# Linear attention and a squared-ReLU MLP on one core: query loads moved up, output stores moved to the SyncE queue, and a margin on every transfer in the kernel's own planner

## The chip, the cores and the metric

The kernel runs on one core of a Trainium2 chip. The time is the device time of one execution in microseconds. The kernel before took 288.01 us, the median of three executions (287.98 to 288.55). One further execution was profiled; it took 291.93 us, and its span in the trace is 290.2 us.

A core has TensorE (matmul, "PE" in the profile, with the weight loads as "PEld"), VectorE ("DVE"), ScalarE ("ACT"), GpSimd ("POOL") and SyncE ("SP", which only issues transfers). Transfers are issued on queues by SyncE, GpSimd or ScalarE, and 16 DMA engines carry them out.

## The reference

Eight batches of eight heads, 576 positions, head size 64. Attention is linear: with r = relu(x), the features of queries and keys are r·cos and r·sin of the position, so no softmax and no 576 x 576 matrix occurs. Then each position's 512 numbers go through an MLP with relu squared.

```python
batch, n_heads, seq, head_dim = (8, 8, 576, 64)

def phi(x, c, s):
    r = np.maximum(x, 0.0)
    return np.concatenate([r * c, r * s], axis=-1)      # 64 -> 128 features
q_p = phi(q, cos_w, sin_w)
k_p = phi(k, cos_w, sin_w)
kv = np.einsum('bhsf,bhsd->bhfd', k_p, v)
z = np.sum(k_p, axis=2)
num = np.einsum('bhsf,bhfd->bhsd', q_p, kv)
den = np.einsum('bhsf,bhf->bhs', q_p, z)[..., None] + 1e-06
attn_out = num / den

x = attn_out.transpose(0, 2, 1, 3).reshape(B * S, H * D)   # 4608 x 512
h = x @ w_in                                               # 512 -> 2048
r = np.maximum(h, 0.0)
return (r * r) @ w_out                                     # 2048 -> 512
```

Inputs and output are float32; the kernel multiplies in bf16.

## The kernel before

A batch has 512 positions in four pieces of 128 (j = 0 to 3) and a tail of 64 (j = 4), which has tensors of its own (kt, vt, qt, kpt, qpTt, xTt and so on). For each batch the steps are:

1. load k, v and q (1 MB each) and their tails;
2. features of k and q on ScalarE and VectorE (kp, qp), and a cast of v (vx);
3. "kz": the product of keys and values on TensorE, into kvz;
4. queries transposed (qp to qpT), from batch 2 on by a DMA transpose on the SyncE queue;
5. "num": qpT times kvz on TensorE, then the division on VectorE, which gives x;
6. x transposed (x to xT), from batch 2 on by a DMA transpose on the SyncE queue;
7. first MLP product (w1), relu and square (gT); from batch 3 on by Strassen's seven products, with sums of blocks in xs, w1s, rs;
8. second MLP product (w2), from batch 2 on (half of batch 1 too) by seven products per pair of row blocks ("pair"), with sums of blocks in gs and w2s, results in ysb;
9. store of ysb.

While TensorE does steps 7 and 8 of one batch, the other engines prepare the next two. Nobody writes that interleaving by hand: the kernel holds a planner. Each operation is declared with the engines that could do it, a guessed cost in us, what it reads and writes, and, for TensorE, a place in time. The planner then runs a list schedule with its guesses, chooses buffers, and emits all instructions in the order found. On the chip each engine takes its own instructions in that order and waits where data are missing.

```python
    def plan(self, t0):
        # (cut: takes, again and again, the operation that can start first)
            o.eng, o.start, o.end = e, s, s + o.engs[e]
            o.done = o.end + (o.lat if o.lat is not None else 0.17 if e == "PE" else 0.09) + self.HOP
            if o.size:                       # a transfer: one pipe for all
                pipe = o.done = max(o.end + o.land, pipe) + o.size
                if o.held is not None:
                    o.end = max(o.end, o.done - o.held)
            clock[e] = o.end
```

`size` is the guessed time of a transfer in the pipe (3.4 us for 1 MB), `land` a guessed latency. Loads, transposes and stores have a size, and so do the four loads of w1, which the hand-written prologue has issued before and which the planner only gets told of:

```python
    given = lambda keys, t, **kw: add(("GIVEN", 0.0), lambda _: None, w=keys, pos=t, **kw)
    for i in range(4):
        given([("w1", i)], 12.2, size=2.6)
    # (cut)
    t0 = {"PE": 16.8, "ACT": 17.3, "DVE": 17.1, "SP": 10.0, "POOL": 20.0, "GIVEN": 0.0}
```

The first operations after the prologue are declared in these lines (batch 0; `declare_plain` is the first MLP product without Strassen, `hb` its block of the hidden layer):

```python
    for j in (2, 3, J):
        for c in "cs":
            declare_feature("q", 0, j, c, DVE1 if c == "c" else ACT1)
        t = {2: 17.5, 3: 18.0, J: 27.0}[j]
        declare_qT_pe(0, j, t, BOTH)
        declare_num(0, j, t + 2.0)
        declare_xT_pe(0, j, t + 4.0, BOTH)
    for s in range(8):
        for i in range(2):
            declare_plain(0, s % 4 * 4 + 2 * i, s // 4, T1[0] + s * 2 * PROD2 + i * PROD2, s == 0)
```

The loads, the attention of batches 4 to 7 and the stores:

```python
    def declare_load(b, nm, eng, pos=None, after=()):
        # (cut) the main part, then the tail, each an operation of the queue `eng`
            add((eng, cost), load, w=[buf], pos=pos, size=size, after=after)

        # in declare_qT: a DMA transpose; `turned` remembers it
        turned["q", b, i] = add(("SP", 1.7 if n == 2 else 1.2), qT, r=keys, w=[dst], land=1.6, held=2.0, ...)

        # in declare_pair: the store of two row blocks, or of two sets of tails
        def store(_):
            if pair < 2:
                put(b, 2 * pair, at(y), n=2, eng=nc.gpsimd)
            else:
                for i in range(2):
                    put_tails(four(b) * 2 + i, at(y)[:, i])
        add(("POOL", 0.6), store, r=keys(0) + keys(1), size=1.7)

    for b in range(2, B):
        # (cut) first MLP product of batch b
        if b + 2 < B:
            for nm in "kv":
                declare_load(b + 2, nm, "SP", after=[turned["q", b + 1, J // 2]])
            declare_load(b + 2, "q", "SP", after=[turned["x", b + 1, J // 2]])
            declare_att(b + 2, T2[b] + 5.5, [T1[b + 1] + 0.3 + 1.75 * j for j in range(NS)])
        for i, pair in enumerate(PAIRS[b]):
            declare_pair(b, pair, T2[b] + i * 7 * PROD2)
```

`declare_att(b, kpos, npos)` gives TensorE's places for kz (`kpos`) and for the five num steps (`npos`). T1[b] and T2[b] are the places where the first and second MLP product of batch b begin. There is one buffer each for k, v and q (and for each tail), two for ysb, two for qpT, four for xT. The very last pair (batch 7, pair 1) stores its four quarters on SyncE (three) and ScalarE (one), in both versions.

Of the kernel before, what the change touches and what calls it, by code (L numbers as in the profile page):

```python
# [19 lines left out]
class Buf:  # L20


    def __init__(self, pool):
        self.pool, self.i, self.users = pool, None, 0
# [10 lines left out]
class Planner:  # L35
# [7 lines left out]

    HOP = 0.07

    def __init__(self, pools, window, in_turn):
        self.in_turn = in_turn
        self.free = {p: [(0.0, i) for i in range(n)] for p, n in pools.items()}
        self.window = window
        self.ops, self.writer, self.readers = [], {}, {}  # L50
        self.turns = {}
# [6 lines left out]
    def add(self, engs, fn, r=(), w=(), pos=None, lat=None, size=None, after=(), land=2.2, held=None):  # L58
        if isinstance(engs, tuple):
            engs = {engs[0]: engs[1]}  # L60
        if size:
            lat = land + size
        op = Op(engs, fn, pos, lat, size)
        op.land, op.held = land, held
        for k in r:
            if k in self.writer:
                op.deps.add(self.writer[k])
            self.readers.setdefault(k, []).append(op)
        for k in w:
            if k in self.writer:  # L70
                op.deps.add(self.writer[k])
            op.deps.update(x for x in self.readers.get(k, ()) if x is not op)
            self.writer[k], self.readers[k] = op, []
        for k in list(r) + list(w):
            b = k[0] if isinstance(k, tuple) else k
            if isinstance(b, Buf) and b not in op.bufs:
                op.bufs.append(b)
                b.users += 1
        op.after = set(after) - op.deps
        op.deps |= op.after  # L80
        self.ops.append(op)
        return op
# [27 lines left out]
    def plan(self, t0):  # L110
        ops = self.ops
        for n, op in enumerate(ops):
            op.n = n
            for d in op.deps:
                d.succ.append(op)
        pe = sorted((o for o in ops if "PE" in o.engs), key=lambda o: (o.pos, o.n))
        t = t0["PE"]
        for o in pe:
            o.late = o.slot = t
            t += o.engs["PE"]  # L120
        for o in reversed(ops):
            d = max(o.engs.values()) + (o.lat or 0.16)
            for s in o.succ:
                o.late = min(o.late, s.late - d)
            if "PE" not in o.engs:
                ends = [
                    s.slot + s.engs["PE"]
                    for s in o.deps
                    if "PE" in s.engs and any(b in s.bufs for b in o.bufs if b.pool in "FB")
                ]  # L130
                if ends:
                    o.late = min(o.late, max(ends) + 1.0)
        clock = dict(t0)
        waiting = {o: len(o.deps) for o in ops}
        pipe = 0.0
        ready = {e: [] for e in clock}
        order = []

        def arm(o):
            for e in o.engs:  # L140
                ready[e].append(o)

        for o in ops:
            if not o.deps:
                arm(o)
        left = len(ops)
        head = 0
        while left:
            best = None
            while head < len(pe) and pe[head].start is not None:  # L150
                head += 1
            for e in clock:
                cand = []
                for o in ready[e]:
                    if e == "PE" and o.slot > pe[head].slot + self.window:
                        continue
                    s = max(clock[e], o.pos if e not in ("PE",) and o.pos else 0.0)
                    for d in o.deps:
                        ordered = d in o.after or d.eng == e and e in ("PE", "ACT", "DVE")
                        s = max(s, d.end if ordered else d.done)  # L160
                    s = self.room(o, s)[0]
                    if s is not None:
                        cand.append((s, o))
                if not cand:
                    continue
                s0 = min(c[0] for c in cand)
                s, o = min(
                    (c for c in cand if c[0] <= s0 + 1e-9),
                    key=lambda c: (c[1].slot if e == "PE" else c[1].late, c[1].n),
                )  # L170
                if best is None or s < best[0]:
                    best = (s, e, o)
            if best is None:
                stuck = [o for o in pe if o.start is None][:6]
                raise RuntimeError(f"stuck: {[(o.fn.__name__, o.pos, o.n) for o in stuck]}")
            s, e, o = best
            for x in o.engs:
                ready[x].remove(o)
            o.eng, o.start, o.end = e, s, s + o.engs[e]
            o.done = o.end + (o.lat if o.lat is not None else 0.17 if e == "PE" else 0.09) + self.HOP  # L180
            if o.size:
                pipe = o.done = max(o.end + o.land, pipe) + o.size
                if o.held is not None:
                    o.end = max(o.end, o.done - o.held)
            clock[e] = o.end
            for b, i in self.room(o, s)[1]:
                b.i = i
                self.free[b.pool] = [f for f in self.free[b.pool] if f[1] != i]
            for b in o.bufs:
                b.users -= 1  # L190
                b.last = max(getattr(b, "last", 0.0), o.done)
                if b.users == 0:
                    self.free[b.pool].append((b.last, b.i))
            for x in o.succ:
                waiting[x] -= 1
                if not waiting[x]:
                    arm(x)
            order.append(o)
            left -= 1
        return order  # L200
# [3 lines left out]
def kernel(  # L204
# [82 lines left out]
    def at(buf, name=None):  # L287
        return mem[name or buf.pool][:, buf.i]
# [67 lines left out]
    def put(b, tt, y, c0=0, c1=DM, eng=None, n=1):  # L356
        dst = bass.AP(
            tensor=out.tensor,
            offset=(b * S + tt) * DM + c0,
            ap=[[J * DM, P], [1, n * DM if n > 1 else c1 - c0]],  # L360
        )
        eng.dma_start(out=dst, in_=y.rearrange("p i c -> p (i c)") if n > 1 else y[:, c0:c1])  # L362

    def put_tails(m, y):
        for i in range(2):
            dst = bass.AP(
                tensor=out.tensor,
                offset=((2 * m + i) * S + MAIN) * DM,
                ap=[[DM, TAIL], [1, DM]],
            )  # L370
            nc.gpsimd.dma_start(out=dst, in_=y[i * TAIL : (i + 1) * TAIL, :])

# [30 lines left out]


    LOAD = 3.4
    T_MM, T_MM128, T_MM65, T_TR = 0.1092, 0.0586, 0.0296, 0.066
    plan = Planner(POOLS, 4.5, ("gs1", "gs2", "gs3", "gs4"))
    add = plan.add  # L410
    PROD1, PROD2 = 4 * T_MM, 8 * T_MM

# [439 lines left out]
    def four(b):  # L852
        return 0 if b < 7 else 1
# [12 lines left out]
    def w2_keys(i, j):  # L866
        return [("w2", 2 * i + n) for n in range(2)]

    def declare_pair(b, pair, t):
        A, Bk, E = plan.buf("F"), plan.buf("B"), plan.buf("F")  # L870
        u = plan.buf("u")
# [61 lines left out]

        def store(_):
            if pair < 2:
                put(b, 2 * pair, at(y), n=2, eng=nc.gpsimd)
            else:
                for i in range(2):
                    put_tails(four(b) * 2 + i, at(y)[:, i])

        add(("POOL", 0.6), store, r=keys(0) + keys(1), size=1.7)

    def declare_rows(b, tiles, t, f_banks):

# [212 lines left out]
    for b in range(2, B):  # L1157
        if b > 2:
            if b in SEVEN:
                declare_x_sums(b)  # L1160
                for r in range(4):
                    declare_seven1(b, r, T1[b] + r * 7 * PROD1)
            for m, first, n in TAILS[b]:
                for i in range(first, first + n):
                    declare_tails(m, 2 * i, T2[b] - 1.5 + 0.01 * i)
        if b + 2 < B:
            for nm in "kv":
                declare_load(b + 2, nm, "SP", after=[turned["q", b + 1, J // 2]])
            declare_load(b + 2, "q", "SP", after=[turned["x", b + 1, J // 2]])
            declare_att(b + 2, T2[b] + 5.5, [T1[b + 1] + 0.3 + 1.75 * j for j in range(NS)])  # L1170
        for i, pair in enumerate(PAIRS[b]):
            declare_pair(b, pair, T2[b] + i * 7 * PROD2)

# [34 lines left out]
```

## Time and profile before

| | before |
|---|---|
| timed executions, median (range) | 288.01 us (287.98 to 288.55) |
| span of the profiled execution | 290.2 us |
| TensorE busy | 273.7 us, 94% |
| VectorE busy | 219.8 us, 76% |
| ScalarE busy | 192.6 us, 66% |
| GpSimd busy | 39.4 us, 14% |
| moved by DMA | 53.02 MB, mean 183 GB/s |
| 1 MB loads on SyncE, median issue to landing: k, v, q | 6.8, 10.2, 6.4 us |
| 512 KB stores on GpSimd, median issue to landing | 4.9 us, 15 of them |
| DMA transposes, median issue to landing: qpT, xT | 6.1, 5.4 us |

How to read the lines that follow. A group line names the source line, the engine, the operation, what it writes and reads (`qpT<-qp`), and how many. In the waits, "PE banks L401 <- DMA qpT<-qp: 4.5, 3, 2.8" says that TensorE's instructions of line 401 (its matmuls, all through one helper) waited for a transfer from qp to qpT: 4.5 us in total, three times, the longest 2.8. In a timeline each line has the start in us, the time it took, the engine, and what it did; a bracket at the end is the idle time of that engine before it and what ended it. SPq is SyncE's queue: the time there is that of issuing, and the transfer lands later.

### The profile page before, as it was taken

What the parts mean: (1) busy time and instruction counts of PE and PEld (TensorE: products, weight loads), DVE (VectorE), ACT (ScalarE), POOL (GpSimd) and SP (SyncE); (2) the same over time, 40 slices, a digit from 0 to 9 for tenths busy, and PEclk for the clock granted to TensorE, in tenths of its full rate; (3) what the DMA queues carried; (4) which work ended last, traced back from release to release, by engine and by line L of the source; (5) the groups of instructions that cost most, each with busy time, mean ns of one, the idle gap of its engine ahead of it and who ended that gap; (6) DMA issues with size and microseconds to landing.
All of it is one profiled execution on the core that took longest, in us unless ns stands there. A gap on an engine that the chain in (4) does not pass through costs nothing.

```text
span 290.2 us, 7068 instructions
## 1 busy us (share of the span) xinstructions
PE 273.7 (94%) x2827; PEld 225.6 (78%) x2827; DVE 219.8 (76%) x512; ACT 192.6 (66%) x379; POOL 39.4 (14%) x67
## 2 busy tenths in 40 slices
PE   8999999999999899589999999997999999999994
PEld 3678755887689788377788888976889888888883
DVE  2859999988845886389977799679974999169661
ACT  4676924897965877459946995689834853585521
POOL 8834345100000000000000000000013000100021
PEclk9999999999999999999999999999999999999999
DMA  7999999799999959999599866998096500110015
GB/s 247 289 207 320 324 242 388 175 171 325 237 189 267 230 163 138 218 312 161 101 189 291 217 188 116 275 288 202 9 224 97 136 3 0 75 72 2 1 75 145
DMA packets 77569, 53.02 MB, mean 183 GB/s; under 512 B 52032, under 2 KB 73024, under 8 KB 77536
## 3 DMA queue, kind: packets, MB, share of 16 engines
q1 hardware_dynamic: 67856, 29.76, 47.6%
q0 software_dynamic: 9536, 22.68, 26.9%
q8 instruction: 22, 0.36, 0.5%
q14 instruction: 11, 0.09, 0.1%
q10 hardware_dynamic: 144, 0.13, 0.1%
HBM read 36.70 MB, written 9.44 MB: 159 GB/s over the span
## 4 chain that ended last, share of the span: by engine, by line
PE 53%; DVE 17%; DMA 16%; POOL 4%; ACT 3%; SPq 3%; issue 3%; DVEq 0%; POOLq 0%; ACTq 0%
PE banks L401 52%; DVE gT L390 6%; DMA kt<-in_k_dram 6%; DMA qt<-in_q_dram 4%; DMA qpT<-qp 4%; DVE rs L393 3%; DMA k<-in_k_dram 2%; DVE gs L398 2%; SPq L329 2%; DVE w1s L398 2%; POOL w1sb L344 1%; DVE qp L379 1%; DVE kp L379 1%; SPq L337 1%; ACT rs L387 1%
## 5 line engine op out<-in xcount | busy, mean ns | idle before, releaser
L401 PEld LDWEIGHTS <-w1sb 128*128 128x128 bf16 x784 | 73.0, 98 | 11.3 <-issue 2.4
L401 PE MATMUL banks<-xT,w1sb 128*128 128x256 bf16 (+1 forms) x576 | 68.4, 267 | 1.0 <-DVE x L599 0.4
L401 PEld LDWEIGHTS <-gs 128*128 128x128 bf16 x480 | 46.5, 98 | 7.4 <-DVE gs L398 1.2
L401 PE MATMUL banks<-w2sb,gT 128*128 128x256 bf16 (+1 forms) x304 | 50.2, 306 | 0.8 <-ACT banks L905 0.5
L401 PEld LDWEIGHTS <-gT 128*128 128x128 bf16 x408 | 38.4, 98 | 13.6 <-issue 1.3
L387 ACT ACTIVATE rt<-banks 128x512 bf16<-128x512 f32 x64 | 37.7, 601 | 14.1 <-PE banks L401 9.4
L362 POOL DMA_DIRECT2D out_dram<-ysb x15 | 8.1, 541 | 213.4 <-DVE ysb L398 92.1
L401 PEld LDWEIGHTS <-w1s 128*128 128x128 bf16 x320 | 30.6, 98 | 7.1 <-issue 3.3
L401 PE MATMUL banks<-w2sb,gs 128*128 128x256 bf16 x240 | 30.9, 273 | 0.4 <-DVE ysb L398 0.4
L393 DVE CUSTOM_DVE_ANT_0 rs<-banks,sums 128x512 bf16<-128x512 f32 x40 | 27.2, 686 | 4.6 <-ACT sums L800 3.6
L401 PE MATMUL banks<-w2s,gs 128*128 128x256 bf16 x240 | 30.0, 273 | 0.5 <-DVE gs L398 0.3
L390 DVE TENSOR_TENSOR gT<-rs 128x1024 bf16<-128x1024 bf16 (+1 forms) x50 | 28.3, 580 | 1.6 <-ACT rs L387 0.8
L390 DVE TENSOR_TENSOR gT<-rt 128x512 bf16<-128x512 bf16 x48 | 19.9, 422 | 12.2 <-ACT rt L387 11.7
L398 DVE TENSOR_TENSOR ysb<-banks,sums 128x256 f32<-128x256 f32 x30 | 12.7, 422 | 19.5 <-ACT sums L914 9.1
L387 ACT ACTIVATE rs<-banks 128x512 bf16<-128x512 f32 x40 | 23.4, 610 | 3.7 <-PE banks L401 3.7
L401 PE MATMUL banks<-xs,w1s 128*128 128x256 bf16 x160 | 23.7, 273 | 0.8 <-ACT banks L793 0.8
L401 PE MATMUL banks<-xT,w1s 128*128 128x256 bf16 x160 | 22.3, 272 | 1.5 <-DVE rs L393 1.5
L377 ACT ACTIVATE qp<-q,sin_col 128x512 bf16<-128x512 f32 x32 | 22.9, 735 | 1.1 <-DMA q<-in_q_dram 1.1
L377 ACT ACTIVATE kp<-k,sin_col 128x512 bf16<-128x512 f32 x32 | 22.7, 738 | 0.2 <-DMA k<-in_k_dram 0.2
L599 DVE TENSOR_TENSOR x<-banks,den 128x512 bf16<-128x512 f32 x30 | 20.7, 692 | 1.0
L398 DVE TENSOR_TENSOR gs<-gT 128x1024 bf16<-128x1024 bf16 x26 | 17.9, 689 | 1.6 <-PE banks L401 1.1
L800 ACT COPY sums<-banks 128x512 f32<-128x512 f32 x20 | 11.9, 593 | 6.4 <-PE banks L401 6.1
(106 smaller groups left out, 377.6 us busy)
## 6 DMA issues: line engine op xcount, KB each, us to landing
out_dram<-ysb POOLq DMA_DIRECT2D x15, 512.0 KB, 4.9
k<-in_k_dram SPq DMA_DIRECT2D x6, 1024.0 KB, 6.8
v<-in_v_dram SPq DMA_DIRECT2D x5, 1024.0 KB, 10.2
q<-in_q_dram SPq DMA_DIRECT2D x5, 1024.0 KB, 6.4
v<-in_v_dram POOLq DMA_DIRECT2D x3, 1024.0 KB, 10.5
w1sb<-in_moe_w_in_dram POOLq DMA_DIRECT2D x4, 512.0 KB, 11.4
w2sb<-in_moe_w_out_dram POOLq DMA_DIRECT2D x4, 512.0 KB, 13.0
q<-in_q_dram POOLq DMA_DIRECT2D x2, 1024.0 KB, 9.5
```

Source lines behind the costliest of these rows:

```text
L329: eng.dma_start(out=main[:, :, js, :], in_=src[b, :, 0:MAIN, :].rearrange("h (p j) d -> p h j d", j=J)[:, :, js, :],)
L337: eng.dma_start(out=tail[g * TAIL : (g + 1) * TAIL, :, :], in_=src[b, g * HH : (g + 1) * HH, MAIN:S, :].rearrange("h p d -> p h d"),)
L362: eng.dma_start(out=dst, in_=y.rearrange("p i c -> p (i c)") if n > 1 else y[:, c0:c1])
L377: nc.scalar.activation(out=dst, in_=src, func=ACTF.Relu, scale=col)
L379: nc.vector.tensor_scalar(out=dst, in0=src, scalar1=0.0, scalar2=col, op0=ALU.max, op1=ALU.mult)
L387: nc.scalar.activation(out=out, in_=in_, func=ACTF.Relu)
L390: nc.vector.tensor_tensor(out=out, in0=in_, in1=in_, op=ALU.mult)
L393: nc.vector._custom_dve(TENSOR_ADD_SAT, out=out, in0=in0, in1=in1, s0=float("inf"), s1=0.0)
L398: nc.vector.tensor_tensor(out=out, in0=in0, in1=in1, op=op)
L401: nc.tensor.matmul(out=out, lhsT=lhsT, rhs=rhs, start=start, stop=stop, skip_group_check=True)
L599: nc.vector.tensor_tensor(out=x_at(b, j).rearrange("p (b k) (l d) -> p b k l d", b=n, l=2), in0=n4[:, :, :, 0:D].rearrange("p b (k l) d -> ...
L800: add(("ACT", 0.5), lambda _: nc.scalar.copy(out=at(u3), in_=bank(Bk)), r=[Bk], w=[u3])
```

## The change

Four things change together. The planner gets a margin: it takes every transfer to be of use 2.0 us later than it would compute, so what depends on a transfer is put later ("care on every transfer"). The queries of batches 4 to 7 are loaded together with keys and values instead of after the last transpose of x of the batch before. The stores of batches 2 to 7 go to the SyncE queue, where loads and transposes stand in line too, instead of to GpSimd's. And the places of kz and num for batches 4 to 7 are written anew: num 2.3 us earlier (LATER = -2.0 in place of +0.3), kz relative to the first product that follows. The aim is that fewer of TensorE's steps wait for a transfer, and that stores don't share the DMA engines with transposes that TensorE needs soon.

```diff
-    def __init__(self, pools, window, in_turn):
+    def __init__(self, pools, window, in_turn, margin):
+        self.margin = margin
@@ in plan
             if o.size:
-                pipe = o.done = max(o.end + o.land, pipe) + o.size
+                pipe = max(o.end + o.land, pipe) + o.size
+                o.done = pipe + self.margin
                 if o.held is not None:
-                    o.end = max(o.end, o.done - o.held)
+                    o.end = max(o.end, pipe - o.held)
@@
-    plan = Planner(POOLS, 4.5, ("gs1", "gs2", "gs3", "gs4"))
+    LATER = -2.0
+    plan = Planner(POOLS, 4.5, ("gs1", "gs2", "gs3", "gs4"), 2.0)
@@
+    def st_name(b):
+        return "SP" if b >= 2 else "POOL"
+    def st_eng(b):
+        return nc.sync if b >= 2 else nc.gpsimd
@@ in declare_pair (put_tails takes the engine too)
-                put(b, 2 * pair, at(y), n=2, eng=nc.gpsimd)
+                put(b, 2 * pair, at(y), n=2, eng=st_eng(b))
-                    put_tails(four(b) * 2 + i, at(y)[:, i])
-        add(("POOL", 0.6), store, r=keys(0) + keys(1), size=1.7)
+                    put_tails(four(b) * 2 + i, at(y)[:, i], st_eng(b))
+        add((st_name(b), 0.6), store, r=keys(0) + keys(1), size=1.7)
@@ in the loop over batches
-            for nm in "kv":
+            for nm in "kvq":
                 declare_load(b + 2, nm, "SP", after=[turned["q", b + 1, J // 2]])
-            declare_load(b + 2, "q", "SP", after=[turned["x", b + 1, J // 2]])
-            declare_att(b + 2, T2[b] + 5.5, [T1[b + 1] + 0.3 + 1.75 * j for j in range(NS)])
+            declare_att(b + 2, T1[b + 1] - 7.5, [T1[b + 1] + LATER + 1.75 * j for j in range(NS)])
```

More of the change, by code (lines that the diff above doesn't have):

```diff
@@ L362, in put, with put_tails @@
         eng.dma_start(out=dst, in_=y.rearrange("p i c -> p (i c)") if n > 1 else y[:, c0:c1])
-    def put_tails(m, y):
+    def put_tails(m, y, eng):
         for i in range(2):
@@ L370, in put_tails @@
             )
-            nc.gpsimd.dma_start(out=dst, in_=y[i * TAIL : (i + 1) * TAIL, :])
+            eng.dma_start(out=dst, in_=y[i * TAIL : (i + 1) * TAIL, :])
     def relu_scale(eng, dst, src, col):
```

## The prediction

> **What bounds the kernel now.** I read the page's first two parts, then the waits of TensorE, then TensorE's timeline around the idle stretches, then what stood on the SyncE queue there. The page first:
>
> ```profile
> PE 273.7 (94%) x2827; PEld 225.6 (78%) x2827; DVE 219.8 (76%) x512; ACT 192.6 (66%) x379; POOL 39.4 (14%) x67
> ...
> PE   8999999999999899589999999997999999999994
> ...
> DMA  7999999799999959999599866998096500110015
> ```
>
> TensorE is busy for 273.7 of 290.2 us, so everything that a schedule can win lies in its 16.5 us of idle time, and some of that is start and end. The holes show in the slices: an 8 and a 5 in slices 16 and 17 (109 to 123 us), a 9 or less near 190 to 200. Which wait ends last there is told by TensorE's own waits:
>
> ```profile
> PE banks L401 <- DMA qpT<-qp: 4.5, 3, 2.8
> PE banks L401 <- DVE rs L393: 1.5, 2, 0.9
> ...
> PE banks L401 <- DMA w1sb<-in_moe_w_in_dram: 0.3, 2, 0.2
> ```
>
> 4.5 us of it, in three waits, is for the transposed queries (qpT), which a DMA transpose on the SyncE queue makes. The timeline of TensorE places them, and places the smaller waits about 20 us earlier:
>
> ```profile
> 98.50 1.91 PE L401 MATMUL banks<-xT,w1sb 128*128 128x256 bf16 x16 [0.41 <-DVE x L599]
> 100.99 0.32 PE L401 MATMUL banks<-kvz,qpTt 128*64 128x65 bf16 x8 [0.59 <-ACT rt L387]
> ...
> 120.19 0.42 PE L401 MATMUL banks<-kvz,qpT 128*128 128x65 bf16 x8 [2.81 <-DMA qpT<-qp]
> ...
> 124.08 0.42 PE L401 MATMUL banks<-kvz,qpT 128*128 128x65 bf16 x8 [1.48 <-DMA qpT<-qp]
> ```
>
> Two holes, 2.81 and 1.48 us, belong to batch 4 alone. (The third, 0.21 us at 150.54, is batch 5's.) The reason stands on the two issuing queues:
>
> ```profile
> 103.87 0.58 SPq L329 DMA_DIRECT2D q<-in_q_dram  x1
> 104.50 1.29 SPq L337 DMA_DIRECT2D qt<-in_q_dram  x2
> 107.40 1.35 SPq L627 DMA_TRANSPOSE xT<-x  x1
> 111.34 8.43 SPq L538 DMA_TRANSPOSE qpT<-qp  x2
> ```
>
> ```profile
> 111.74 0.53 POOL L362 DMA_DIRECT2D out_dram<-ysb  x1 [24.63 <-ACT sums L909]
> 117.51 0.53 POOL L362 DMA_DIRECT2D out_dram<-ysb  x1 [5.24 <-DVE ysb L398]
> ```
>
> The queries of batch 4 are asked for only at 103.87 and land at about 110; their features are ready at 111.3; and 0.4 us after the first transpose is issued, GpSimd issues a 512 KB store of batch 2 on another queue. By the trace's landings this store took 8.2 us (the median is 4.9), the first transpose 8.8 us and the second 10.6 us (median 6.1). Batch 6, whose store was issued after both transposes, had 4.5 and 4.8 us and no hole.
>
> **What the Trainium skill says.** "DMA: Bandwidth & Descriptors", section "Queues, rings and completion order": a DMA engine takes turns between the queues that have work for it, a packet at a time, and takes one queue's descriptors in their order. Section "Issuing engines are not separate DMA queues" of the same page: whoever issues, the same 16 engines do the work and the transfers interleave. The trace agrees: store and transposes of batch 4 were both slow while they overlapped. On one queue the store would start behind or ahead of the transposes. "Perfetto Trace Analysis", section "Summary: the profiler window per engine type": for a DMA issued by SyncE the slice is generation and push, not the movement; the trace agrees (slices of 0.58 us, landing 6.4 us later), so I go by landings.
>
> **The change part by part.** The kernel's planner decides the order, so I read the built order of both versions. TensorE's instructions are the same in number and kind; only their order differs. I count places in TensorE work (8 matmuls of 128x256 take 0.87 us in the timeline, 8 of 128x65 take 0.24), from 16.8 us on.
>
> *Queries with keys and values.* In the old order the load of q for batches 4 to 7 may be issued 11 to 19 us of TensorE work after those of k and v, with 4.6 us left until VectorE comes to the first q feature of batch 4. In the new order it stands next to k and v, with 16.3 us. For batch 3 the old kernel already does so: k issued at 64.22, all three tensors with tails landed by 78.25, 14.0 us. So the wait on late queries goes. In its place the tails of k and v, which stand behind q, land about 3.2 us later (k and v of batch 4 landed 3.2 us apart, 1 MB each). Against this VectorE reaches the tail of k later: 96.3 to 99.4 for batch 4, 178.6 to 181.7 for batch 7. Net near zero for batch 4; for batch 7, whose loads are also issued 2 us earlier, some gain, because there the tail at 194.9 us held VectorE 0.9 us, and TensorE lost 0.78 and 0.90 us at 199.7 and 201.2 behind it. I put 0.6 us on batch 4 (half of 0.41 + 0.59 + 0.16) and 1.0 on batch 7.
>
> *Stores on SyncE.* 19 transfers move, 11 of 512 KB and 8 tails of 128 KB. GpSimd issued them at 0.53 us each and is otherwise idle, so taking them off it wins nothing. On SyncE the two stores of batch 2, 3 and 4 stand together behind the transposes of x and ahead of the next batch's query transposes, 12 us of TensorE work or more before them, and 3 to 10 us after TensorE has made their data: SyncE should not stand still for them, and they no longer meet the transposes. The two ysb buffers come free later, but the next pair writes them more than 15 us of work later. At the end four tail stores are issued on SyncE just before the last stores; the last one of all is on ScalarE (issued at 287.25), so nothing is lost.
>
> *The numerators and the margin.* LATER puts the numerators 2.3 us earlier, the 2 us margin holds them back behind their transposes. From the place where the first transpose of q may be issued to the first numerator there are now 8.3, 10.8, 9.0 and 15.2 us for batches 4 to 7 (before 7.9, 8.1, 8.1, 13.1). In the trace the issue came 2 to 3 us after that place and an undisturbed transpose took 4.5 to 6.1 us: 6.5 to 9 us. So the 2.81 + 1.48 + 0.21 = 4.5 us should go nearly whole, as the store is out of the way: I take 4.3.
>
> *The start.* The margin also falls on the four w1 loads, of which the planner knows only a guessed time. It believes w1 2 us later, and so puts the query transposes of pieces 2 and 3 of batch 0 before the first up-projection. But w1's first quarter was there at 16.24 us, and the transposes wait for ScalarE's features at about 17.6 and 18.3. In the old trace TensorE did 24 matmuls of 128x128 by then (24 x 0.0586 = 1.41 us) and ended the transposes at 18.86. In the new order it ends them at about 18.75 with those 24 still to do: 1.3 us lost. The 0.19 + 0.15 us waited for w1 later go: 1.0 us net loss, and TensorE is busy without a hole from there to 98 us but for 0.22 us, so it stays.
>
> Sum in the profiled run: -4.3 - 0.6 - 1.0 + 1.0 = -4.9 us. But the timed runs are at 288.01 while the profiled execution took 291.93, 3.9 us more. Some of the profile's waits must then be shorter or absent in the timed runs, those on transfers most likely. I count half of the three gains, 2.95 us, against the 1.0 lost, and leave 0.4 us for new small waits of a new order: 288.0 - 2.95 + 1.0 + 0.4 = 286.4. With the gains whole it is 288.0 - 4.9 + 0.4 = 283.5. I settle between, nearer to the first: 285.6.
>
> **The rivals.** (a) The stores become the bound of SyncE: each waits in line, and everything behind it waits too. For: the queue's own instructions already take 1.2 to 6 us per transpose, and issuing the two tails of k 2.2 to 4.1 us, so the queue is crowded around each load. Against: the built order has them after their data by 3 to 10 us of TensorE work (batches 2 to 4). It would give back 2 to 4 us: 288 to 290. (b) The tails of k land too late with q before them, and VectorE, which works in order, stands still with squares behind the tail feature: up to 2 us in each of batches 4 to 7, 290 or more. Against: the 3.1 us by which the feature is placed later. (c) The hole at 120 us is a thing of the profiled run. Then the change only costs its start: 288.5 to 289. (d) VectorE and ScalarE set the pace in 130 to 210 us (busy 9 or more of 10 us in several stretches), so holes that close at 120 open later as waits for rs and banks: gain 1 us, 287.
>
> **Range and chances.** The middle case is 285.6; (d) and half of (c) give the upper end 288.2, the gains whole 283.5, with luck 283.2. Faster by over 2% needs under 282.3, which asks for 5.7 us where the waits that the change touches come to some 7 us in all, less the start: 6%. Slower by over 2% needs 293.8, which only (a) and (b) together reach: 2%.
>
> **What would show it.** Right: no wait of TensorE for qpT over 0.5 us; landings of the query transposes at 4.5 to 6.5 us for batches 4 to 7; the first w1 matmul after about 18.7 us instead of 16.2; stores on SyncE issued with no wait of SyncE for y. Wrong: SyncE waiting for ysb before a transpose, VectorE waiting for kt or q by more than 1.5 us, or the hole before batch 4's numerators still there.

## The result, and the profile after

The changed kernel takes 283.94 us (median of four executions, 283.72 to 285.48) against 288.19 us of the kernel before, measured beside it (287.98 to 288.55). The ratio is 0.9863, with a 95% interval of 0.9826 to 0.990: 1.4% faster. The profiled execution of the kernel before took 291.93 us, 3.9 us more than the timed ones, so its two holes at 120 us need not be a part of the 288.19.

The page of the changed kernel, its first two parts:

```profile
PE 271.0 (96%) x2827; PEld 225.5 (80%) x2827; DVE 218.2 (77%) x513; ACT 191.0 (68%) x378; POOL 30.6 (11%) x48
...
PE   8889999999999989999999999998999999999994
...
DMA  7999999698999978996599948993835400300024
```

TensorE is busy for 271.0 of 282.0 us; its idle time fell from the 16.5 us of the longer profiled execution to 11.0 us, and the 5 and the 8 of slices 17 and 18 (116 to 131 us) are gone. Its busy time fell too, by 2.7 us (from 273.7; it is 273.5 in e1 below, which has the old order), with the same 2827 matmuls: part of what an order costs stands in the time that the profile calls busy. TensorE's waits name what is left of the idle time:

```profile
PE banks L554 <- ACT qp L379: 1.3, 1, 1.3
...
PE banks L403 <- ACT rt L389: 1.1, 1, 1.1
PE banks L403 <- DVE vx L386: 0.8, 1, 0.8
PE banks L403 <- DVE rs L395: 0.6, 1, 0.6
```

No transfer is among them; line 554 is the transpose of queries at the start, which is new. SyncE's queue around the place of the old holes:

```profile
108.36 4.36 SPq L541 DMA_TRANSPOSE qpT<-qp  x2
112.88 1.72 SPq L541 DMA_TRANSPOSE qpTt<-qpt  x1
114.66 0.58 SPq L331 DMA_DIRECT2D k<-in_k_dram  x1
...
131.07 1.46 SPq L364 DMA_DIRECT2D out_dram<-ysb  x2
```

Batch 4's transposes now come 3 us earlier, and the two stores of batch 2 go out at 131 us, after the transposes of x and before the next queries. The times from issue to landing of the qpT transposes, first before, then after:

```profile
DMA to landing us min/median/max: 4.5/6.1/10.6
```

```profile
DMA to landing us min/median/max: 4.2/4.5/6.0
```

So far everything looks as predicted. The experiments say something else about why.

### The profile page after: what moved, and what is told of

Its sections match the earlier page's. It is cut to its first block, busy times and chain, and to the rows that moved or that the text cites. A ratio compares the mean times of both kernels' runs of the same rounds, so it can differ in the third digit from the quotient of the medians.

```text
span 282.0 us, 7065 instructions
## 1 busy us (share of the span) xinstructions
PE 271.0 (96%) x2827; PEld 225.5 (80%) x2827; DVE 218.2 (77%) x513; ACT 191.0 (68%) x378; POOL 30.6 (11%) x48
## 4 chain that ended last, share of the span: by engine, by line
PE 81%; DVE 7%; ACT 6%; DMA 3%; issue 2%; POOL 0%; ACTq 0%; DVEq 0%; POOLq 0%
PE banks L403 78%; DMA v<-in_v_dram 2%; DVE gs L400 2%; DVE gT L392 2%; PE banks L554 1%; ACT rs L389 1%; DMA xTt<-xt 1%; ACT rt L389 1%; DVE x L602 1%; ACT kp L379 1%; DVE rs L395 1%; DVE qp L381 1%; PE banks L642 1%; PE banks L1104 1%; ACT sums L803 1%
## 5 line engine op out<-in xcount | busy, mean ns | idle before, releaser
L403 PE MATMUL banks<-xT,w1sb 128*128 128x256 bf16 (+1 forms) x576 | 67.6, 267 | 0.0
L389 ACT ACTIVATE rs<-banks 128x512 bf16<-128x512 f32 x40 | 22.8, 605 | 4.1 <-PE banks L403 4.1
L403 PE MATMUL banks<-xTt,w1sb 128*128 128x256 bf16 x128 | 15.6, 272 | 0.0
L381 DVE TENSOR_SCALAR kp<-k,cos_col 128x512 bf16<-128x512 f32 x25 | 11.8, 505 | 4.7 <-DMA k<-in_k_dram 4.7
## 6 DMA issues: line engine op xcount, KB each, us to landing
v<-in_v_dram POOLq DMA_DIRECT2D x3, 1024.0 KB, 10.6
w1sb<-in_moe_w_in_dram POOLq DMA_DIRECT2D x4, 512.0 KB, 10.6
q<-in_q_dram POOLq DMA_DIRECT2D x2, 1024.0 KB, 10.6
```

The lines of the kernel that those rows point to most:

```text
L381: nc.vector.tensor_scalar(out=dst, in0=src, scalar1=0.0, scalar2=col, op0=ALU.max, op1=ALU.mult)
L389: nc.scalar.activation(out=out, in_=in_, func=ACTF.Relu)
L403: nc.tensor.matmul(out=out, lhsT=lhsT, rhs=rhs, start=start, stop=stop, skip_group_check=True)
```

## The experiments

The experiments were measured in three sets (e1 to e4, e5 to e8, e9 to e12), the change before them. All ratios are to the kernel before, measured in the same set; its medians were 288.2 to 288.8 us, so differences of half a microsecond between sets mean nothing. Medians and ratios leave out executions over 1.5% longer than the fastest of the same kernel in the set: 35 of 108 of the kernel before, one of e7's four, three of e9's 20, and none of the 20 each of e1, e4, e6 and e8.

| kernel | median us | ratio, 95% interval |
|---|---|---|
| the change | 283.94 | 0.986 (0.983 to 0.990) |
| e1 before, stores of batch 2 left out | 289.18 | 1.002 (0.999 to 1.005) |
| e2 change, its stores issued by GpSimd | 286.17 | 0.982 (0.975 to 0.990) |
| e3 change, no margin on w1 | 284.42 | 0.976 (0.969 to 0.984) |
| e4 before + margin | 290.46 | 1.006 (1.003 to 1.009) |
| e5 before + early q | 292.51 | 1.013 (1.009 to 1.018) |
| e6 before + stores on SyncE | 287.69 | 0.996 (0.993 to 0.998) |
| e7 before + new places | 293.01 | 1.013 (1.003 to 1.022) |
| e8 change, old places of kz and num | 287.80 | 0.998 (0.995 to 1.001) |
| e9 change, old place of num | 288.39 | 0.999 (0.996 to 1.002) |
| e10 change, old place of kz | 284.72 | 0.982 (0.975 to 0.989) |
| e11 change, margin 0 | 286.51 | 0.989 (0.982 to 0.996) |
| e12 change, late q | 286.00 | 0.988 (0.982 to 0.993) |

e2, e3 and e10 to e12 have four executions each, e7 has three, and their intervals are wider; for those I compare medians of the same set rather than ratios.

The hand-written start, which is the same in all kernels, takes a different time in each trace: TensorE's first kz matmul comes at 10.15 us in the trace of the change and between 10.19 us (e8) and 12.01 us (e11) in those of its variants. From there to the end of the span the change takes 271.8 us, e3 271.6, e10 271.8, e12 272.5, e2 273.0, e11 273.8 and e8 275.8. Where traces are compared below, these times are better than the spans.

### e1: do the stores make the holes?

```diff
         def store(_):
+            if b == 2:
+                return
```

The stores of batch 2 are left out, so that part of the output is never written. The order on TensorE, VectorE, ScalarE and SyncE is that of before.

> The kernel before with its two stores of batch 2 left out and nothing else moved (that part of the output is not written). Theory A, the stores collide with batch 4's query transposes: these land in 4.5 to 6.5 us instead of 8.8 and 10.6, TensorE's holes of 2.81 and 1.48 us shrink to under 1.0 us together, and the timed runs gain 1.5 to 4 us on 288.2. Theory B, the late load of q alone makes the holes: the first transpose is still issued near 111 us, the holes stay over 2.5 us together and the time is within 1 us of 288.2.

The transposes were issued at 111.62, as before (111.34), and now took 4.36 us to issue instead of 8.43. They landed after 4.4 and 4.7 us instead of 8.8 and 10.6.

```profile
111.62 4.36 SPq L538 DMA_TRANSPOSE qpT<-qp  x2
```

TensorE waited for no transpose in this trace. But the time is 289.18 (20 executions, 287.93 to 291.97), the same as before (1.002). So theory A is right about the trace and wrong about the time, and theory B falls too, as the late q alone made no hole. In the executions compared, taking away the cause of these holes wins nothing that can be measured. Whether they are absent there is not shown: the only trace of the kernel before is that of the longer execution.

### e2: the changed order, stores issued by GpSimd

```diff
     def st_eng(b):
-        return nc.sync if b >= 2 else nc.gpsimd
+        return nc.gpsimd
```

The planner still believes in SyncE, so all compute engines keep their order to the last instruction.

> The changed kernel with every engine's order as it is, and only the 13 stores of batches 2 to 7 issued by GpSimd again, so that each goes out as soon as its data are there. Theory A, the collision is what mattered: batch 4's query transposes meet the stores of batch 2 again and land in 7 to 10 us, TensorE waits 1 to 3 us for them, and the time is 285 to 287. Theory B, the early q and the new places are what mattered: the landings go up by 1 us at most and the time stays within 0.7 us of 283.9.

286.17 us, against 284.42 of e3 in the same set and 283.94 of the change: by the medians the stores' queue is worth 1.7 to 2.2 us. The spans of the two traces differ by 2.4 us, but 1.3 of that stand before any of the moved stores, where the first kz waits for the cast of v. First the change, then e2:

```profile
10.15 1.33 PE L403 MATMUL banks<-vx,kp 128*128 128x65 bf16 x32 [0.75 <-DVE vx L386]
```

```profile
11.47 1.27 PE L403 MATMUL banks<-vx,kp 128*128 128x65 bf16 x32 [2.07 <-DVE vx L386]
```

From there on e2 loses 1.2 us. It doesn't lose them through the transposes: they landed in 4.2 to 6.4 us, and TensorE waited for none. The waits of ScalarE from 140 to 166 us have two lines that the changed kernel doesn't have there:

```profile
ACT vx L386 <- DMA v<-in_v_dram: 0.9, 1, 0.9
...
ACT kp L379 <- DMA k<-in_k_dram: 0.6, 1, 0.6
```

Two stores were issued at 144.51 and 150.69 beside the loads of k and v of batch 6, issued at 145.55 and 146.90. By the trace's landings k took 7.5 us instead of 5.6 and v 10.3 instead of 8.7. ScalarE stood in line for them, and TensorE behind ScalarE:

```profile
155.88 0.60 PE L403 MATMUL banks<-xs,w1s 128*128 128x256 bf16 x4 [0.69 <-ACT banks L796]
158.41 0.60 PE L403 MATMUL banks<-xT,w1s 128*128 128x256 bf16 x4 [0.19 <-ACT sums L800]
```

With a third wait of 0.18 us at 160.49 that is 1.06 us, about what e2 loses after its start. Theory A has the time right and the victim wrong: what TensorE pays for are the next loads.

### e3: the start

```diff
-                o.done = pipe + self.margin
+                o.done = pipe + (0.0 if e == "GIVEN" else self.margin)
```

> The changed kernel without the margin on the four w1 loads, which alone puts the transposes of batch 0's pieces 2 and 3 back behind the first up-projections. My theory of the start: the hole of 1.30 us before the first transposes goes, two waits for w1 of 0.15 to 0.2 us come back, and the time is 282.5 to 283.3. Rival: the start has slack that is taken up later by VectorE's pace at 25 to 42 us, and the time stays at 283.9 within 0.4.

The loss at the start is real, and removing it wins nothing that the medians show. The timelines of TensorE, first of the changed kernel, then of e3:

```profile
17.79 1.23 PE L554 MATMUL banks<-ident,qp 128*128 128x128 bf16 x16 [1.30 <-ACT qp L379]
```

```profile
16.80 0.61 PE L403 MATMUL banks<-xT,w1sb 128*128 128x128 bf16 x8
17.63 1.05 PE L403 MATMUL banks<-xT,w1sb 128*128 128x128 bf16 x16 [0.23 <-ACT xT L386]
18.52 1.06 PE L554 MATMUL banks<-ident,qp 128*128 128x128 bf16 x16
...
101.67 0.32 PE L403 MATMUL banks<-kvz,qpTt 128*64 128x65 bf16 x8 [1.45 <-DVE x L602]
```

The hole of 1.30 us is gone, e3 begins its last numerator of batch 0 at 31.8 us (the change at 32.6), but at kz of batch 1 the lead is 0.3 us (41.8 and 42.1), and at kz of batch 4 nothing (103.7 in both): there the wait for VectorE or ScalarE at 101.7 us is 1.45 us instead of 1.10. (e3's first kz came 0.5 us later than the change's, so its true lead is that much larger.) The median, 284.42, shows no gain. The rival is right about the time: more than half of the lead is taken up by 104 us, and from the first kz to the end e3 takes 271.6 us, the change 271.8.

### e4 to e7: each part alone

e4 adds the margin to the planner of before as in the diff of the change, with nothing else. e5:

```diff
-            for nm in "kv":
+            for nm in "kvq":
                 declare_load(b + 2, nm, "SP", after=[turned["q", b + 1, J // 2]])
-            declare_load(b + 2, "q", "SP", after=[turned["x", b + 1, J // 2]])
```

e6 takes the store lines of the change alone, and e7 the line of the places:

```diff
-            declare_att(b + 2, T2[b] + 5.5, [T1[b + 1] + 0.3 + 1.75 * j for j in range(NS)])
+            declare_att(b + 2, T1[b + 1] - 7.5, [T1[b + 1] - 2.0 + 1.75 * j for j in range(NS)])
```

> The kernel before with the 2 us margin alone; q is still loaded late and stores stay on GpSimd. Theory A (collision) and theory B (late q): the start costs 1.0 us, and the order gives batch 4's numerators hardly more room, so holes for qpT of 1 to 4 us stay: 287.5 to 289.5. Theory C, the margin is what mattered: the waits for qpT go, 284 to 285.5.

> The kernel before with q of batches 4 to 7 loaded together with k and v, and nothing else. Theory Q, the late q made ScalarE and VectorE do the q features in a hurry beside the k features of the next batch, and TensorE waited for both: the waits for rs, sums and banks at 120 to 200 us shrink by 2 us or more and the time is 285 to 286.5. Theory M, early loads help only together with the margin, as without it the tails of k, now behind q, hold VectorE: waits of VectorE for kt over 2 us, 287.5 to 289.

> The kernel before with the stores of batches 2 to 7 on SyncE, and nothing else. Theory S, stores away from transposes: no execution near 292 or above any more, and 287 to 288.2. Rival, SyncE stands in line for the data of a store: SyncE waits for ysb in the middle of the loads or transposes, the holes before the numerators grow, 289 to 292.

> The kernel before with the new places of kz and num of batches 4 to 7, and nothing else. Theory Q and M: without early loads and the margin the numerators come too soon, TensorE waits 1 us or more for qpT in batches 4 to 6: 288.5 to 291. Rival, the places alone make the gain: 284 to 286.

Only the stores win by themselves (287.69, as theory S had it; the longest execution took 290.4 us). SyncE does wait 2.8 us for the data of a store at 110 us in e6's trace, as the rival had it, but TensorE has no wait for batch 4's qpT behind it. Margin, early q and places each lose.

e4 lost a little more than expected, and not to qpT (one wait of 0.26 us): besides the start, its timeline has waits of 0.50 and 1.00 us for ScalarE at 131 and 133 us and 0.63 for VectorE at 136.5.

e5 fits neither theory. ScalarE's timeline shows the main loss:

```profile
120.72 0.57 ACT L793 COPY banks<-banks 128x512 f32<-128x512 f32 x1
124.97 0.72 ACT L377 ACTIVATE kp<-k,cos_col 128x512 bf16<-128x512 f32 x1 [3.68 <-DMA k<-in_k_dram]
125.60 0.57 ACT L800 COPY sums<-banks 128x512 f32<-128x512 f32 x1
```

The planner put the first key feature of batch 5 where it believed k to be there. k was issued at 117.14 beside a store (116.84), took 7.8 us, and ScalarE, whose next instruction in order this feature was, stood idle for 3.68 us with the copies of sums behind it; TensorE lost 3.18 us behind them at 126.2. That is the case for which the margin is made; that the margin prevents it was not tried on e5.

e7 did what theories Q and M said, and more of it. TensorE's timeline:

```profile
120.98 0.42 PE L401 MATMUL banks<-kvz,qpT 128*128 128x65 bf16 x8 [2.09 <-DMA qpT<-qp]
...
157.35 0.32 PE L401 MATMUL banks<-kvz,qpTt 128*64 128x65 bf16 x8 [1.19 <-DMA qpTt<-qpt]
160.36 0.72 PE L401 MATMUL banks<-xs,w1sb 128*128 128x256 bf16 x4 [2.15 <-ACT sums L800]
```

Here the early numerators, without early queries and without the margin, wait for their transposes.

### e8 to e10: the places

e8 is the change with the old line of places, e9 with LATER = 0.3 alone, e10 with the old place of kz (T2[b] + 5.5) alone.

> The changed kernel with the old places of kz and num, so margin, early q and stores on SyncE together. Theory Q and M: the places are trimming, and the time is 283.5 to 285.0. Rival, the places carry a part of their own: 285.5 to 287.

> The changed kernel with num of batches 4 to 7 back at its old place (2.3 us later) and the new place of kz. Theory N: VectorE and ScalarE are full in the second half of each first MLP product, and earlier numerators let VectorE divide in the first half, where it has room. Then the waits for rs, gs and ysb at the ends of the first products come back: 286 to 288. Theory K, it is kz of batch 7 (6.5 us later in the new places) that counts: 284 to 285.

> The changed kernel with kz back at its old place and num at the new one. Theory N: 284 to 285. Theory K: waits of TensorE of 1 us or more in 190 to 210 us, 286 to 288.

My theory that the places are trimming fell with e8: at 287.80 the other three parts together win nothing that can be told from zero. e9 and e10 say which place it is. With the old place of num the time is 288.39; with the old place of kz, in the same set, it is 284.72. Without the 2.3 us by which the numerators move, the gain is gone. No other values of LATER were run, so how much of this is the distance and how much a lucky order of the planner is not shown. What follows rests on e8's trace.

What differs, the windows show. Three stretches of 8 us over batch 4's first MLP product and the start of its second, first of the changed kernel, then of e8, where that product begins 2.3 us later (148.86 us instead of 146.58). Columns: stretch, its length, busy us of TensorE, weight loads, VectorE, ScalarE and GpSimd, then clock, DMA share and GB/s:

```profile
145.00:153.00 8.00, 8.00 (x97) 7.04 (x94) 6.93 (x21) 5.65 (x12) 0.00 (x0) 1.00 1.00 308
153.00:161.00 8.00, 7.99 (x74) 6.97 (x72) 7.46 (x15) 7.98 (x17) 0.00 (x0) 1.00 1.15 211
161.00:169.00 8.00, 7.99 (x101) 6.73 (x100) 7.90 (x16) 8.00 (x19) 0.00 (x0) 1.00 0.52 150
```

```profile
147.30:155.30 8.00, 8.00 (x98) 7.03 (x97) 5.71 (x15) 6.33 (x12) 0.00 (x0) 1.00 1.10 367
155.30:163.30 8.00, 8.00 (x76) 7.17 (x74) 7.89 (x17) 7.87 (x16) 0.00 (x0) 1.00 1.06 236
163.30:171.30 8.00, 7.17 (x91) 5.51 (x89) 7.76 (x16) 7.73 (x18) 0.00 (x0) 1.00 0.41 35
```

In both, VectorE and ScalarE are nearly full in the second and third stretch. In e8 VectorE has 2.3 us of room in the first (5.71 of 8), of which the changed kernel uses half (6.93), and TensorE's loss in the third stretch, 0.83 us, is gone. The first stretch of the products of batches 3, 5 and 6, placed in the same way, shows the same with smaller differences: VectorE is busy 6.16, 6.97 and 6.69 us in the changed kernel and 5.67, 6.29 and 6.02 us in e8. What moved into the room are, for the most part, divisions that follow the numerators. The same stretches for the division's line alone (busy us and number on VectorE), the changed kernel first:

```profile
145.00:153.00 8.00, 3.19 (x5) 1.00 1.00 308
153.00:161.00 8.00, 0.00 (x0) 1.00 1.15 211
```

```profile
147.30:155.30 8.00, 2.44 (x4) 1.00 1.10 367
155.30:163.30 8.00, 0.75 (x2) 1.00 1.06 236
```

In e8's timeline of TensorE waits for VectorE stand at the end of the product, here of batches 4 and 5:

```profile
165.15 0.60 PE L403 MATMUL banks<-xT,w1s 128*128 128x256 bf16 x4 [0.49 <-DVE rs L395]
168.07 1.92 PE L403 MATMUL banks<-w2s,gs 128*128 128x256 bf16 x16 [0.33 <-DVE gs L400]
...
196.06 0.60 PE L403 MATMUL banks<-xT,w1s 128*128 128x256 bf16 x4 [0.49 <-DVE rs L395]
198.79 1.92 PE L403 MATMUL banks<-w2s,gs 128*128 128x256 bf16 x16 [0.28 <-DVE gs L400]
```

The changed kernel has none of batch 4's two waits, but it has waits of 0.58 and 0.38 us in batch 5. Over the whole profile the waits that TensorE's timeline names after 16 us come to 7.8 us in e8 and 4.7 in the changed kernel; the spans are 286.0 and 282.0, and most of the rest is TensorE's busy time (272.1 and 271.0). That later divisions make VectorE late, and VectorE TensorE, is read from this one pair of traces; no run moved the divisions alone.

### e11 and e12: does the early numerator need the margin and the early q?

e11 has a margin of 0.0 in place of 2.0; e12 loads q late again, as before, in the changed kernel.

> The changed kernel with a margin of 0. Theory M, early numerators need the margin, or they stand before their transposes have landed: waits for qpT of 1 us or more in total, 286 to 290, though the start is 1.0 us shorter. Rival, early q alone gives the transposes time enough: no wait for qpT over 0.5 us, 282.5 to 284.5.

> The changed kernel with q of batches 4 to 7 loaded late again. Theory Q, early numerators need an early q: the planner, which knows the load, must put the numerators later or TensorE waits for qpT: 286.5 to 290. Rival, the planner finds another order as good: 284 to 285.5.

Both cost time: 286.51 and 286.00, against 284.72 of e10 in the same set (1.8 and 1.3 us) and 283.94 of the change (2.6 and 2.1 us); by the traces, from the first kz on, they lose 2.0 and 0.7 us. Neither loses them by long waits for qpT, of which e11 has one of 0.16 us and e12 one of 0.22. In e12 the planner, which knows that q is late, puts batch 4's first numerator at 119.7 us instead of 115.5 (1.4 us of the difference is e12's later start), so the divisions are late again, and VectorE is late at the end of the product:

```profile
119.69 0.89 PE L403 MATMUL banks<-kvz,qpT 128*128 128x65 bf16 x16 [0.22 <-DMA qpT<-qp]
...
135.22 0.60 PE L403 MATMUL banks<-xT,w1s 128*128 128x256 bf16 x4 [0.49 <-DVE rs L395]
137.42 0.39 PE L403 MATMUL banks<-w2sb,gT 128*128 128x256 bf16 x2 [0.46 <-DVE gT L392]
138.14 1.92 PE L403 MATMUL banks<-w2s,gs 128*128 128x256 bf16 x16 [0.33 <-DVE gs L400]
```

In e11 the start is without its hole, but TensorE waits 1.49 us for ScalarE at 103.3 (1.10 at 101.7 in the change) and 0.71 us for rs at 196.2 (0.58 at 192.6). That the whole margin is worth about 2 us is shown; by which transfer is not. e3 says that it isn't the part on w1.

## Why the prediction was right, and where it was right for the wrong reason

The measured 283.94 us lies in the predicted range (283.2 to 288.2, middle 285.6). By the steps of the prediction:

- *The holes for qpT go (4.3 us, half counted).* The landings came as predicted, 4.2 to 6.0 us, and no wait for qpT is left. The size is wrong: e1 shows that taking away their cause wins nothing that can be measured in the time compared (1.002). This is the step that failed. Rival (c), the hole as a thing of the profiled run, was right on it, but not on what follows from it (288.5 to 289). The warning was there, 3.9 us between the profiled and the timed executions, and I took half of it into account instead of all.
- *Queries with keys and values.* Not a gain by itself (e5: 4 us slower), but a part of the whole: without it the change gives back 1.3 to 2.1 us by the medians and 0.7 us in the trace (e12). The reason given, a wait on late queries, is not what is lost: e12's trace has no wait for qpT longer than 0.22 us.
- *Stores on SyncE.* Worth 1 us alone (e6) and 1.7 to 2.2 us by the medians in the change (e2). That transfers of different issuers share the 16 engines and interleave, as the Trainium skill has it ("DMA: Bandwidth & Descriptors", section "Issuing engines are not separate DMA queues"), holds in e2's landings (k took 7.5 us beside stores instead of 5.6); but the victim I named was wrong: TensorE paid for the next batch's loads, not for the transposes, although one of these was slowed too (6.4 us instead of 4.3). Rival (a), SyncE standing in line for a store, hardly came: SyncE waited up to 0.9 us before the stores of batches 2 to 4 and once 4.2 us, at 204 us, before stores of tails, and no wait of TensorE for a transfer followed.
- *The numerators.* The prediction describes the 2.3 us and gives them no term in its sum. They are what the gain hangs on: without them 288.39 (e9). Rival (d) names VectorE and ScalarE as the pace at 130 to 210 us; I took that as a limit on the gain and not as the thing that an earlier numerator relieves.
- *The start.* Measured 1.30 us as predicted (1.3); but it is hardly a term of the sum, as e3 shows: without it the time is no shorter, and more than half of the lead is gone by 104 us. "So it stays" was wrong.
- *Rival (b)*, VectorE standing still for the tails of k: no such wait reaches TensorE in the changed kernel, but the like of it happened in e5, on ScalarE, where the margin was missing.
- *The premise.* "Everything that a schedule can win lies in its 16.5 us of idle time" was too narrow: TensorE's busy time fell by 2.7 us between the two profiles. The row of slices was also read one place off (the 5 and the 8 are slices 17 and 18), but nothing rests on it, as the timeline gives the times.

That the middle of the range came within 1.7 us of the measured time is in part luck: two terms that were too large, the holes and the start, stand on opposite sides, and the missing term for the numerators filled the rest.

## What to carry to other kernels

A change made of several parts couldn't be priced part by part here, with a scheduler between them: three of four parts lose alone, the three without the new places win nothing together, and each but kz's place and the margin on w1 is worth 1.3 us or more in the whole, by the medians. Look for the stretch in which the helping engines are full and for the one before it in which they have room, and ask which input lets work move forward into it; then give that input's transfers the time to be safe. And before a hole in a profile is counted as gain, compare the profiled execution with the timed ones: if it is longer by about the size of the hole, the hole may be its own.

## What the runs showed of the hardware that I had not expected

Two 512 KB stores on one queue beside 1 MB loads on another cost the loads about 1.6 to 1.9 us each in e2 (5.6 to 7.5 and 8.7 to 10.3 us from issue to landing). In the same trace the transpose of batch 4's queries that was issued at 112.14, just before a store (112.75), took 6.4 us instead of the 4.3 us of the changed kernel. That is a loss of the same size, but TensorE came to these queries only after they had landed.
